# A fused attention and expert kernel: one group of transposes per attention step, ninth key blocks transposed later, separate accumulators for the experts

## The chip, the cores and the metric

The kernel runs on one NeuronCore of a Trainium2 chip. The metric is device time in microseconds of one launch, the median of several runs. TensorE (PE, with its weight loads as PEld), VectorE (DVE), ScalarE (ACT), GpSimd (POOL) and the DMA queue of SyncE (SP) each run their own instruction stream in order and wait for each other by semaphores. Results of TensorE go to PSUM, which has banks of 512 fp32 columns for each of 128 partitions.

## The reference

```python
# attention: q, k, v are [4, 8, 576, 64]
scores = q @ k.T / 8 + bias(log-distance MLP of w1, b1, w2)   # per head
attn = softmax(scores)            # minus row max, over sum + 1e-9
x = (attn @ v) -> [2304, 512]
# 8 experts, every token goes to its argmax expert
h = relu(x[mask] @ w1[e]); y = h @ w2[e]
out[mask] = gate_w * sigmoid(x @ w_output_gate)[e] * y
# gated feed-forward on all tokens
g = x @ w_gate; out = (silu(g) * (x @ w_val)) @ w_out         # d_ff = 1536
```

## The kernel before

The program has four stages, one after the other: the position bias is made and stored to DRAM (to 68 us), attention (68 to 331 us), the experts (331 to 597 us), the feed-forward (597 us to the end). The recording order in the code is the order on each engine; nothing reorders it but TensorE's own pulling ahead of weight loads.

**Attention** runs 16 *units*, a unit being a pair of heads p of a batch b. A unit has five *steps* c = 0 to 4, each for a tile of 128 query rows of both heads; c = 4 has the last 64 rows of both heads in one tile. Keys are 576 = four and a half blocks of 128. Written without head, one step n does this:

- `s_pe` (L242): the scores S of step n, three fp32r products for each half of the keys; for c < 4 two heads in two PSUM tiles of the pool `pS` (tag `S`, two buffers in all), for c = 4 one tile.
- `s_max` (L255, VectorE): scores plus bias from PSUM into the SBUF tile E (tag `ph`, four buffers), with the row minimum of the negated sum; `s_exp` (L260, ScalarE): the exponentials, in place.
- `t_pe` (L279): transposes of E of step n-2 ("old") into the PSUM tile T, two banks, one for each half of the partitions; 64-row transposes in pairs, one pair for each block of 128 columns. `t_ev` (L295): the copy from T into the SBUF tiles `pt`, which the weighted sums read.
- the weighted sums `pv` (L349, from `pv_list`), spread over steps by `PVA` and `PVB`; `bc_recip` (L328) spreads the reciprocal row sums at c = 1 and c = 3; at c = 2 and c = 0 VectorE multiplies (L355).

E has nine blocks of 128 for two heads of 576 columns; the fifth of them (number 4) is the one that holds the end of one head and the beginning of the other, and is written to place 8 of `pt`. Here it is called the ninth block. The order of a step is set by the loop at L860:

```python
            if old:
                t_both(*old, 0)      # first group: blocks 0 to 3, copied by VectorE
            E = ap.tile([128, 2 * S], F32, tag="ph", bufs=4, name="E")
            sc = s_pe(p, b, c)
            if old:
                t_both(*old, 1)      # second group: blocks 5 to 8 and 4, copied by ScalarE
```

Both groups use the same columns of both banks of T, so that the second waits for VectorE's copy of the first and the first of the next step for ScalarE's copy of the second. At c = 4 the ninth block needs a GpSimd copy of 64 columns first (L899).

**The experts** loop over 64 steps: `h_step` (L549) makes hidden values in one bank of T, taken in turn by `t_tile` (L266), ScalarE and VectorE split them into a high and a low part (L558, L559), and `y_step` (L561) multiplies the ones of the step before, 12 matmuls each. On TensorE the order is h(n+1), y(n), h(n+2), y(n+1). In between, as listed per step (`todo`), the weights of the next expert are converted (L517, L519) and the first weights of the feed-forward (L941 to L952). `q_h` (L666) also uses T.

Of the kernel before, what the change touches and what calls it, by code (L numbers as in the profile page):

```python
# [9 lines left out]
F32 = mybir.dt.float32  # L10
F32R = mybir.dt.float32r
# [5 lines left out]
PSUM = bass.MemoryType.PSUM  # L17
# [3 lines left out]
B, H, S, D = 4, 8, 576, 64  # L21
# [87 lines left out]
def body(tc, qt, kt, va, vb, ws, moe_w_gate, moe_w_output_gate, moe_w1, moe_w2, w_gate, w_val, w_out, ctab, cst, cst2, out):  # L109
    nc = tc.nc  # L110
    with ExitStack() as ctx:
        const = ctx.enter_context(tc.tile_pool(name="const", bufs=1))
        dram = ctx.enter_context(tc.tile_pool(name="dram", bufs=1, space=DRAM))
        att = ExitStack()
        pers = ctx.enter_context(tc.tile_pool(name="pers", bufs=1))
        vw = att.enter_context(tc.tile_pool(name="vw", bufs=1))
        ap = att.enter_context(tc.tile_pool(name="att", bufs=1))
        rt = att.enter_context(tc.tile_pool(name="rt", bufs=1))
        pS = att.enter_context(tc.tile_pool(name="pS", bufs=2, space=PSUM))
        pO = att.enter_context(tc.tile_pool(name="pO", bufs=1, space=PSUM))  # L120
# [9 lines left out]
        reps = ap.tile([32, 256], F32, tag="ph", bufs=4, name="reps")  # L130
# [21 lines left out]
        for r in range(4):  # L152
            o = slice(32 * r, 32 * r + 32)
# [86 lines left out]
        pts = {}  # L240
# [22 lines left out]
        tt = pO.tile([128, 2, 512], F32, name="T")  # L263
        turn = [0]

        def t_tile():  # L266
            turn[0] ^= 1
            return tt[:, turn[0] ^ 1]

        def pv_tile(i, name):  # L270
            return pO.tile([128, 512], F32, tag=f"pv{i}", bufs=1, name=name)
# [4 lines left out]
            swap[0] ^= 1  # L276
            return pv_tile(swap[0] ^ 1, name)

        def t_pe(E, c, i):  # L279

            ns = ((0, 1, 2, 3), (5, 6, 7, 8, 4) if c < 4 else (4,))[i]
            for j, n in enumerate(ns):
                for r in range(2):
                    k, o = slice(64 * r, 64 * r + 64), 128 * n + (64 * r if c == 4 and i == 0 else 0)
                    nc.tensor.transpose(tt[:, r, 64 * j:64 * j + 64], E[k, o:o + 128], ident[k, k])  # L287
# [7 lines left out]
        def t_ev(p, b, c, i):  # L295

            pt = pts[p, b][c // 2 if c < 4 else 1]
            if c < 4:
                o, n = 128 * (c % 2), 4 + i
                copy(i, pt[:, 4 * i:4 * i + n, o:o + 128].rearrange("p n (r t) -> p r n t", r=2),  # L300
                     tt[:, :, 0:64 * n].rearrange("p r (n t) -> p r n t", n=n))
            elif i == 0:
                copy(i, pt[:, 0:8, 256:320].rearrange("p (r n) t -> p r n t", r=2), tt[:, :, 0:256].rearrange("p r (n t) -> p r n t", n=4))
            else:
                for r in range(2):
                    k = slice(64 * r, 64 * r + 64)
                    copy(i, pt[k, 8, 256:320], tt[k, r, 0:64])

        def t_both(p, b, c, E, i):
            t_pe(E, c, i)  # L310
            t_ev(p, b, c, i)
# [53 lines left out]
        act = vm[:, 0:1]  # L365
# [140 lines left out]
        def conv_w(raw, f, later=None):  # L506

            a, c = raw
            if f < 4:
                ta = ap.tile([128, 2, 4, 128], F32R, tag="ph", bufs=4, name="w1hl")  # L510
# [299 lines left out]
        def z_mm(cnt):  # L810
            c, k = BLKS[cnt]
            act = ZACT[cnt % len(ZACT)]
            zs = zss.pop(cnt)
            pt = pS.tile([128, 1024], F32, tag="S", name="bps")
            ps = [pt[:, 0:512], pt[:, 512:1024]]
            for gq in range(4):
                nc.tensor.matmul(ps[0][32 * gq:32 * gq + 32, 0:512], w2bd, zs[gq][:, 0:512], start=True, stop=True)
            for gq in range(4):
                nc.tensor.matmul(ps[1][32 * gq:32 * gq + 32, 0:64], w2bd, zs[gq][:, 512:576], start=True, stop=True)
            ob = ap.tile([128, S], F32, tag="ph", bufs=4, name="ob")  # L820
# [38 lines left out]
        sts = {}  # L859
        for n, (ui, c) in enumerate(steps):  # L860
            p, b = units[ui]
            g = 9 * ui + min(2 * c + 1, 8)
            if c == 0:
                if b == 0:
                    xT[p] = pers.tile([128, NTOK], F32, tag=f"xT{p}", name=f"xT{p}")
                    if p + 1 < NP:
                        dmaq += [(9 * ui + BL[i], f) for i, f in enumerate(load_bias(p + 1))]
                if b == 1 and p + 1 < NP:
                    dmaq += [(9 * ui + VL[i], f) for i, f in enumerate(load_v(p + 1, nc.sync))]
                if ui + 2 < len(units):  # L870
                    dmaq += [(9 * ui, f) for f in load_u(*units[ui + 2])]
# [12 lines left out]
            old = prev.pop(0) if len(prev) == 2 else None  # L884
            if old:
                t_both(*old, 0)
            E = ap.tile([128, 2 * S], F32, tag="ph", bufs=4, name="E")
            sc = s_pe(p, b, c)
            if old:
                t_both(*old, 1)  # L890
            fs = pe.pop(n, [])
            for f in fs[0:1]:
                f()
            for hh in range(1 if c == 4 else 2):
                e = E[:, S * hh:S * hh + S]
# [17 lines left out]
            prev.append((p, b, c, E))  # L913
# [390 lines left out]
```

## Time and profile before

| | |
|---|---|
| runs | 1055.15 us median of 3 (1054.14 to 1056.36) |
| profiled execution | 1057.95 us, its span 1056.1 us |
| TensorE busy | 1007.4 us (95%), weight loads 798.8 us (76%) |
| VectorE, ScalarE, GpSimd busy | 574.0 us (54%), 449.8 us (43%), 128.6 us (12%) |
| mean granted clock | 0.987 |

The span runs from the first to the last instruction in the profile. Matmuls overlap in their records, so TensorE's busy share holds time in which it starts nothing; the idle time of the weight loads (PEld), with what ended it, shows these waits better.

### The profile page before, as it was taken

The page shows a single profiled execution, that of the slowest core. Times are in us where ns is not written, and L with a number is a line of the kernel's source. Part 1 is how long each engine was busy: PE and PEld are TensorE (multiplying, and loading weights), DVE is VectorE, ACT ScalarE, POOL GpSimd, SP SyncE. Part 2 cuts the span into 40 slices and gives each one's busy share as a digit, 9 for nine tenths or more (in the row PEclk, how much of TensorE's full clock was granted, in tenths as well). Part 3 has the DMA queues.
Part 4 walks back from the last instruction along what each step waited for, and adds up shares of the span by engine and source line. Part 5 has one row for each costly group of instructions (what it writes and reads, how often), then busy time and mean ns, then how long its engine had stood idle before and what let it go on. Part 6 is the DMA issues. An engine that isn't in the chain of part 4 may idle for free. (4 is left out here: it accounts for less than half of the span.)

```text
span 1056.1 us, 18793 instructions
## 1 busy us (share of the span) xinstructions
PE 1007.4 (95%) x7461; PEld 798.8 (76%) x7461; DVE 574.0 (54%) x1241; ACT 449.8 (43%) x931; POOL 128.6 (12%) x138
## 2 busy tenths in 40 slices
PE   6979999999989999999999899999999999999998
PEld 2346666666657899998988677778888888888897
DVE  8966777677666644444556399962223222322322
ACT  6766777676755433333425355541112111211221
POOL 3662343344220000000000000000000000000000
PEclk9988999999999999999999999999999999999999
DMA  6783233342013042724724555512001000200010
GB/s 190 205 263 118 93 100 98 109 133 93 14 36 116 23 161 102 255 97 129 261 100 146 170 160 179 172 58 70 1 1 52 29 1 1 60 1 0 12 30 20
DMA packets 67755, 101.90 MB, mean 96 GB/s; under 512 B 9136, under 2 KB 37936, under 8 KB 67664
## 3 DMA queue, kind: packets, MB, share of 16 engines
q1 hardware_dynamic: 67504, 100.41, 29.8%
q8 instruction: 59, 0.97, 0.4%
q10 hardware_dynamic: 160, 0.26, 0.1%
q14 instruction: 32, 0.26, 0.1%
HBM read 74.63 MB, written 26.03 MB: 95 GB/s over the span
## 5 line engine op out<-in xcount | busy, mean ns | idle before, releaser
L1199 PE MATMUL v<-x,w 128*128 128x512 f32 (+1 forms) x720 | 161.3, 371 | 3.8 <-DVE w L952 3.8
L1199 PE MATMUL g<-x,w 128*128 128x512 f32 (+1 forms) x720 | 159.9, 371 | 2.3 <-DVE xl L707 2.2
L1199 PEld LDWEIGHTS v<-x,w 128*128 128x128 f32 x720 | 125.3, 189 | 32.0 <-DVE w L952 7.5
L1199 PEld LDWEIGHTS g<-x,w 128*128 128x128 f32 x720 | 127.4, 189 | 27.3 <-ACT x L1154 2.5
L1221 PE MATMUL o<-w,uh 128*128 128x512 f32 x432 | 133.3, 390 | 0.0
L1202 DVE TENSOR_TENSOR t<-g,t 128x512 f32<-128x512 f32 (+1 forms) x60 | 38.2, 636 | 170.1 <-ACT t L1201 170.1
L261 ACT ACTIVATE E<-E,st 128x576 f32<-128x576 f32 x144 | 109.9, 766 | 5.1 <-DVE st L256 4.5
L256 DVE CUSTOM_DVE_ANT_0 E<-S,bias 128x576 f32<-128x576 f32 x128 | 92.0, 755 | 16.2 <-PE S L252 8.0
L1201 ACT ACTIVATE t<-g 128x512 f32<-128x512 f32 (+1 forms) x60 | 33.2, 553 | 153.7 <-PE g L1199 153.7
L349 PE MATMUL pv<-pt,rawv 128*64 128x256 f32 (+1 forms) x640 | 97.6, 425 | 0.0
L1206 ACT ACTIVATE uh<-t 128x512 fp32r<-128x512 f32 (+1 forms) x60 | 35.4, 590 | 145.6 <-DVE t L1203 145.6
L1221 PEld LDWEIGHTS o<-w,uh 128*128 128x128 f32 x432 | 80.3, 188 | 16.1
L287 PEld LDWEIGHTS T<-ident,E 64*128 64x128 f32 x1312 | 55.9, 142 | 46.8 <-ACT pt L291 20.2
L293 DVE COPY pt<-T 128x512 f32<-128x512 f32 x80 | 55.2, 691 | 60.8 <-PE T L287 39.6
L291 ACT ACTIVATE pt<-T 128x640 f32<-128x640 f32 (+1 forms) x96 | 52.2, 543 | 74.9 <-PE T L287 74.7
L1221 PE MATMUL o<-w,ul 128*128 128x512 f32 x216 | 84.0, 389 | 0.0
L287 PE MATMUL T<-ident,E 64*128 64x64 f32 x1312 | 77.1, 238 | 6.6 <-ACT pt L291 1.6
L252 PE MATMUL S<-kh,qz 64*128 64x288 f32 (+1 forms) x576 | 77.3, 322 | 3.7 <-DVE st L256 3.1
L558 ACT ACTIVATE qz<-T 128x288 fp32r<-128x288 f32 x63 | 25.9, 411 | 107.0 <-PE T L556 104.9
L559 DVE SCALAR_TENSOR_TENSOR qz<-T,qz 128x288 fp32r<-128x288 f32 x63 | 28.7, 456 | 72.7 <-ACT qz L558 72.4
L1203 DVE TENSOR_TENSOR t<-v,t 128x512 f32<-128x512 f32 (+1 forms) x60 | 38.3, 638 | 54.4 <-PE v L1199 53.0
L556 PE MATMUL T<-xh,whl 128*128 128x288 f32 x256 | 58.2, 302 | 6.4 <-DVE qz L559 5.1
(245 smaller groups left out, 1655.7 us busy)
## 6 DMA issues: line engine op xcount, KB each, us to landing
raww<-in_moe_w_dram SPq DMA_DIRECT2D x16, 768.0 KB, 6.2
bscr<-ob SPq DMA_DIRECT2D x36, 288.0 KB, 4.0
bias<-bscr SPq DMA_DIRECT2D x16, 576.0 KB, 4.2
rw<-in_w_gate_dram SPq DMA_DIRECT2D x12, 512.0 KB, 3.7
rw<-in_w_val_dram SPq DMA_DIRECT2D x12, 512.0 KB, 3.6
rw<-in_w_out_dram SPq DMA_DIRECT2D x12, 512.0 KB, 3.7
rawq<-in_qt_dram SPq DMA_DIRECT2D x16, 320.0 KB, 3.3
rawk<-in_kt_dram SPq DMA_DIRECT2D x16, 288.0 KB, 3.1
```

Of the source, the lines that this page charges most:

```text
L252: nc.tensor.matmul(t[:, f, 0:288], x[k, a], y[k, o], start=i == 0, stop=i == 2)
L256: nc.vector.tensor_tensor_reduce(out=E.rearrange("p (a b) -> p a b", a=2), in0=ps[:, :, 0:288], in1=bt[p, hh, c].rearrange("p (a b) -> p a ...
L261: nc.scalar.activation(E, E, AF.Exp, bias=st[:, 2 * c + hh:2 * c + hh + 1], scale=-1.0, accum_out=st[:, 10 + 2 * c + hh:11 + 2 * c + hh])
L287: nc.tensor.transpose(tt[:, r, 64 * j:64 * j + 64], E[k, o:o + 128], ident[k, k])
L291: nc.scalar.activation(o, x, AF.Copy)
L293: nc.vector.tensor_copy(o, x)
L349: nc.tensor.matmul(st["ps"][64 * hh:64 * hh + 64, 0:w], vt[p][:, hh, b, c, :], pts[p, b][f][:, c + 4 * hh if c < 4 else 8, :], start=c == ...
L556: nc.tensor.matmul(ps, wa[:, x, k], xs[k][y][:, o], start=k == 0 and i == 0, stop=k == 3 and i == 2)
L1199: nc.tensor.matmul(t, a[:, 128 * k:128 * k + 128], x, start=k == 0 and n == 0, stop=k == 3 and n == 2)
L1202: nc.vector.tensor_tensor(t, ps[0], t, ALU.mult)
L1203: nc.vector.tensor_tensor(t, ps[1], t, ALU.mult)
L1221: nc.tensor.matmul(ops[j][m], u[:, o], w, start=f == 0 and n == 0, stop=f == NF - 1 and n == 2)
```

## The change

Per step the scores now come first, then all transposes of the old step in one group of 16 (c < 4), then the weighted sums. ScalarE's copy of blocks 5 to 8 is recorded right behind the group, VectorE's of blocks 0 to 3 behind `s_max`. The ninth blocks of c = 0 and 1 are transposed in the group of c = 2 (four transposes more) into a second PSUM tile `Tx`, taken from the pool `pS`, since the step at whose place this happens (c = 4) needs only one score tile; those of c = 2 and 3 in the group of c = 4. The GpSimd copy is gone: the ninth block of c = 4 is made by one 64x64 transpose and one 64x64 matmul with the identity. `E` is now allocated behind the transposes, so that four buffers still do; `EB` is 4. Behind attention T is given back and the experts take two separate tiles of one bank each.

```diff
@@ s_pe and transposes of one step
-        def t_pe(E, c, i):
-            ns = ((0, 1, 2, 3), (5, 6, 7, 8, 4) if c < 4 else (4,))[i]
-            for j, n in enumerate(ns):
-                for r in range(2):
...
+        def t_blk(E, t, at, n, shift=0):
+            for r in range(2):
+                k, o = slice(64 * r, 64 * r + 64), 128 * n + shift * r
+                nc.tensor.transpose(t[:, r, at:at + 64], E[k, o:o + 128], ident[k, k])
+
+        def t_pe(c, Es, x):
+            t, E = tb["t"], Es[-1]
+            if c == 2:
+                for i in range(2):
+                    t_blk(Es[i], x, 64 * i, 4)
+            if c < 4:
+                for j, n in enumerate((0, 1, 2, 3, 5, 6, 7, 8)):
+                    t_blk(E, t, 64 * j, n)
+            else:
+                for i in range(2):
+                    t_blk(Es[2 + i], t, 256 + 64 * i, 4)
+                for j in range(4):
+                    t_blk(E, t, 64 * j, j, 64)
+                nc.tensor.transpose(t[0:64, 0, 384:448], E[0:64, 512:576], ident[0:64, 0:64])
+                nc.tensor.matmul(t[64:128, 0, 384:448], E[64:128, 0:64], ident[64:128, 64:128], start=True, stop=True)
...
+                copy(act, pt[c // 2][:, n:n + 4, o:o + 128].rearrange("p n (r t) -> p r n t", r=2),
+                     t[:, :, 64 * n:64 * n + 256].rearrange("p r (n t) -> p r n t", n=4))
+                if c == 2 and not act:
+                    copy(0, pt[0][:, 8].rearrange("p (c r t) -> p r c t", c=2, r=2), x[:, :, 0:128].rearrange("p r (c t) -> p r c t", c=2))
...
         def t_tile():
             turn[0] ^= 1
-            return tt[:, turn[0] ^ 1]
+            if "pool" in tb:
+                return tb["pool"].tile([128, 512], F32, tag="T", bufs=2, name="T")
+            return tb["t"][:, turn[0] ^ 1]
...
-            if old:
-                t_both(*old, 0)
-            E = ap.tile([128, 2 * S], F32, tag="ph", bufs=4, name="E")
             sc = s_pe(p, b, c)
             if old:
-                t_both(*old, 1)
-            fs = pe.pop(n, [])
-            for f in fs[0:1]:
+                x = pS.tile([128, 2, 512], F32, tag="S", name="Tx") if c == 4 else None
+                t_pe(old[3], old[4], x)
+                t_ev(*old[1:4], x, 1)
+            E = ap.tile([128, 2 * S], F32, tag="ph", bufs=EB, name="E")
...
                 s_max(p, hh, c, sc[hh], e, st)
                 s_exp(e, st, hh, c)
-            if c == 4:
-                nc.gpsimd.tensor_copy(E[:, 576:640], E[:, 0:64])
...
+            if old:
+                t_ev(*old[1:4], x, 0)
...
+        pT.close()
+        tb["pool"] = att.enter_context(tc.tile_pool(name="pT2", bufs=1, space=PSUM))
```

On TensorE, at the change from the step c = 4 of one unit to c = 0 of the next, the program before reads so (T transposes, S scores, pv weighted sums, pt the copies; a wait stands behind the first instruction that has it):

```order
L287 MATMUL T<-ident,E 128x64 [waits DVE_49]
L287 MATMUL T<-ident,E 128x64 x9
L349 MATMUL pv<-pt_2882,rawv 64x320 x2
L349 MATMUL pv<-pt_3115,rawv 64x256 [waits Activation_49]
L349 MATMUL pv<-pt_3115,rawv 64x256
L287 MATMUL T<-ident,E 128x64 [waits Activation_49]
L287 MATMUL T<-ident,E 128x64 x7
L252 MATMUL S<-kh,qz_117 128x288 [waits Pool_49]
L252 MATMUL S<-kh,qz_117 128x288 [waits DVE_49]
```

and the changed one so:

```order
L288 MATMUL Tx<-ident,E 128x64 [waits DVE_49]
L288 MATMUL Tx<-ident,E 128x64 x3
L288 MATMUL T<-ident,E 128x64 [waits DVE_49]
L288 MATMUL T<-ident,E 128x64 x15
L364 MATMUL pv<-pt_2892,rawv 64x320 x2
L364 MATMUL pv<-pt_3126,rawv 64x256 [waits Activation_49]
L364 MATMUL pv<-pt_3126,rawv 64x256
L255 MATMUL S<-kh,qz_120 128x288 [waits DVE_49,Pool_49]
L255 MATMUL S<-kh,qz_120 128x288 [waits DVE_49,PE_49]
```

The scores of the next unit stand directly behind the weighted sums, and their second matmul, that of the other head, now waits for VectorE and TensorE, since it takes the buffer that `Tx` had.

On VectorE, the same place (L256 and L259 are `s_max`, L293 and L311 the copies out of T; the second L256 or L259 row is the reading of its minimum), before:

```order
L256 ISA E,st<-S,bias 128x576 [waits PE_49]
L256 ISA st 128x1
L293 COPY pt_2882<-T 128x2x4x64 [waits PE_49,Activation_49]
L256 ISA E,st<-S,biast 128x576 [waits PE_49]
L256 ISA st 128x1
L293 COPY pt_2882<-T 128x2x4x64 [waits PE_49,Activation_49]
```

and changed:

```order
L259 ISA st 128x1
L311 COPY pt_2891<-T 128x2x4x64 [waits Activation_49]
L259 ISA E,st<-S,biast 128x576 [waits PE_49]
L259 ISA st 128x1
L311 COPY pt_2892<-T 128x2x4x64 [waits Activation_49]
L311 COPY pt_2891<-Tx 128x2x2x64
```

VectorE's copy out of T, which stood ahead of `s_max`, stands behind it; it waits for ScalarE alone, so for ScalarE's copy of the same group, which itself waits for the group; and a copy out of `Tx` is new behind it.

On TensorE in the expert stage, the end of an h, the y behind it and the beginning of the next h (L556 and L571 are in `h_step`, L569 and L584 in `y_step`), before:

```order
L556 MATMUL T<-xh,whl 128x288
L569 MATMUL y<-qz_118,w2hl 128x288 [waits Activation_49]
L569 MATMUL y<-qz_118,w2hl 128x288 x11
L556 MATMUL T<-xh,whl 128x288 [waits DVE_49]
L556 MATMUL T<-qz_115,whl 128x288
```

and changed:

```order
L571 MATMUL T<-xh,whl 128x288
L584 MATMUL y<-qz_120,whl 128x288 [waits Activation_49]
L584 MATMUL y<-qz_120,whl 128x288 [waits DVE_49]
L584 MATMUL y<-qz_120,whl 128x288 x10
L571 MATMUL T<-xh,whl 128x288
L571 MATMUL T<-qz_118,whl 128x288
```

The wait for VectorE has moved from the first matmul of h to the second of y.

## Rows read from the trace of the kernel before

**Rows 1.** Window of attention: its us, then busy us (count) of each engine, granted clock, DMA share, GB/s.

```profile
90.00:290.00 200.00, 197.78 (x2374) 133.41 (x2368) 141.86 (x352) 142.46 (x342) 75.34 (x97) 1.00 0.31 94
```

**Rows 2.** Waits of the weight loads, same stretch: total us, times, longest.

```profile
PEld T L287 <- DVE pt L293: 12.0, 52, 0.5
...
PEld T L287 <- POOL rw L323: 4.0, 13, 0.3
```

**Rows 3.** TensorE groups by form, same stretch: busy us, mean ns | idle us before.

```profile
L287 PE MATMUL T<-ident,E 64*128 64x64 f32 x1066 | 60.8, 234 | 2.2 <-DVE pt L293 0.2
```

**Rows 4.** Timeline of one step, c=2, all engines: start, us, engine, line.

```profile
245.88 0.47 PE L287 MATMUL T<-ident,E 64*128 64x64 f32 x8
...
246.16 0.51 PE L252 MATMUL S<-kh,qz 64*128 64x288 f32 x4
...
246.46 0.69 DVE L293 COPY pt<-T 128x512 f32<-128x512 f32 x1 [0.80 <-PE T L287]
...
247.20 0.39 PEld L287 LDWEIGHTS T<-ident,E 64*128 64x128 f32 x10 [0.25 <-DVE pt L293]
247.21 0.52 PE L287 MATMUL T<-ident,E 64*128 64x64 f32 x10
...
247.66 1.30 PE L349 MATMUL pv<-pt,rawv 128*64 128x320 f32 x8
247.77 0.70 ACT L291 ACTIVATE pt<-T 128x640 f32<-128x640 f32 x1 [0.65 <-PE T L287]
```

**Rows 5.** The same timeline: a unit's first row, its step c=4, the next unit's first.

```profile
240.09 0.46 PE L287 MATMUL T<-ident,E 64*128 64x64 f32 x8
...
252.43 0.46 PE L287 MATMUL T<-ident,E 64*128 64x64 f32 x8
...
252.82 0.53 PE L252 MATMUL S<-kh,qz 128*128 128x288 f32 x2
...
253.00 0.69 DVE L293 COPY pt<-T 128x512 f32<-128x512 f32 x1 [1.22 <-ACT E L261]
...
253.80 0.39 PEld L287 LDWEIGHTS T<-ident,E 64*128 64x128 f32 x10 [0.17 <-DVE pt L293]
...
254.25 1.19 PE L349 MATMUL pv<-pt,rawv 128*64 128x320 f32 x8
...
255.38 0.46 PE L287 MATMUL T<-ident,E 64*128 64x64 f32 x8
```

**Rows 6.** ScalarE groups by form, attention (90 to 290 us): busy us, mean ns.

```profile
L291 ACT ACTIVATE pt<-T 128x640 f32<-128x640 f32 x52 | 36.7, 706 | 51.4 <-PE T L287 51.4
...
L337 ACT ACTIVATE rb<-rps 128x256 f32<-128x256 f32 x13 | 5.0, 384 | 0.3
```

**Rows 7.** VectorE groups by form, the same stretch.

```profile
L293 DVE COPY pt<-T 128x512 f32<-128x512 f32 x65 | 44.9, 691 | 49.5 <-PE T L287 33.1 <-ACT E L261 14.9 <-ACT rb L337 1.6
...
L355 DVE TENSOR_TENSOR xT<-pv,rb 128x256 f32<-128x256 f32 x13 | 5.5, 419 | 0.0
```

**Rows 8.** Waits of TensorE, 331 to 600 us: total us, times, longest.

```profile
PE T L556 <- DVE qz L559: 5.1, 4, 2.3
...
PE T L671 <- DVE qs L676: 2.1, 3, 1.0
```

**Rows 9.** Timeline of the expert stage, at its longest waits.

```profile
380.61 0.63 ACT L517 ACTIVATE w2hl<-raww 128x512 fp32r<-128x512 f32 x1 [1.45 <-DMA raww<-in_moe_w_dram]
...
382.39 0.41 PE L556 MATMUL T<-xh,whl 128*128 128x288 f32 x1 [1.30 <-DVE qz L559]
...
437.73 0.40 PE L556 MATMUL T<-xh,whl 128*128 128x288 f32 x1 [1.19 <-DVE qz L559]
...
532.72 0.40 PE L556 MATMUL T<-xh,whl 128*128 128x288 f32 x1 [2.27 <-DVE qz L559]
```

**Rows 10.** Windows at the clock's low stretches, columns as in rows 1.

```profile
312.10:319.00 6.90, 6.70 (x48) 4.41 (x50) 4.07 (x12) 3.84 (x10) 0.00 (x0) 0.51 0.70 216
534.00:537.40 3.40, 3.40 (x17) 3.40 (x16) 1.96 (x4) 0.41 (x1) 0.00 (x0) 0.50 0.85 292
```

More of the change, by code (lines that the diff above doesn't have):

```diff
@@ L35 @@
 LG = (1, 5, 5, 7, 8, 10, 10)
+EB = 4
 N0, PRE, FL, LEAD = 6, 3, 0, 0
@@ L120, in body @@
         pO = att.enter_context(tc.tile_pool(name="pO", bufs=1, space=PSUM))
+        pT = ExitStack()
+        pT1 = pT.enter_context(tc.tile_pool(name="pT1", bufs=1, space=PSUM))
         sched = ExitStack()
@@ L129, in body @@
         w_s = const.tile([32, 10], F32, name="w_s")
-        reps = ap.tile([32, 256], F32, tag="ph", bufs=4, name="reps")
+        reps = ap.tile([32, 256], F32, tag="ph", bufs=EB, name="reps")
         rep_sb, w2rep = reps[:, 0:128], reps[:, 128:256]
@@ L261, in s_exp @@
             nc.scalar.activation(E, E, AF.Exp, bias=st[:, 2 * c + hh:2 * c + hh + 1], scale=-1.0, accum_out=st[:, 10 + 2 * c + hh:11 + 2 * c + hh])
-        tt = pO.tile([128, 2, 512], F32, name="T")
+        tb = {"t": pT1.tile([128, 2, 512], F32, name="T")}
         turn = [0]
@@ L277, in pv_next @@
             return pv_tile(swap[0] ^ 1, name)
-        def t_pe(E, c, i):
-            ns = ((0, 1, 2, 3), (5, 6, 7, 8, 4) if c < 4 else (4,))[i]
-            for j, n in enumerate(ns):
-                for r in range(2):
-                    k, o = slice(64 * r, 64 * r + 64), 128 * n + (64 * r if c == 4 and i == 0 else 0)
-                    nc.tensor.transpose(tt[:, r, 64 * j:64 * j + 64], E[k, o:o + 128], ident[k, k])
+        def t_blk(E, t, at, n, shift=0):
[17 more added lines that the diff above has]
+                nc.tensor.matmul(t[64:128, 0, 384:448], E[64:128, 0:64], ident[64:128, 64:128], start=True, stop=True)
         def copy(act, o, x):
@@ L293, in copy, with t_ev @@
                 nc.vector.tensor_copy(o, x)
-        def t_ev(p, b, c, i):
-            pt = pts[p, b][c // 2 if c < 4 else 1]
+        def t_ev(p, b, c, x, act):
+            t, pt = tb["t"], pts[p, b]
             if c < 4:
[L299 to L303, printed above, removed]
-            else:
[L305 to L311, printed above, removed]
+                o, n = 128 * (c % 2), 4 * act
+                copy(act, pt[c // 2][:, n:n + 4, o:o + 128].rearrange("p n (r t) -> p r n t", r=2),
+                     t[:, :, 64 * n:64 * n + 256].rearrange("p r (n t) -> p r n t", n=4))
+                if c == 2 and not act:
+                    copy(0, pt[0][:, 8].rearrange("p (c r t) -> p r c t", c=2, r=2), x[:, :, 0:128].rearrange("p r (c t) -> p r c t", c=2))
+            elif act:
+                copy(1, pt[1][:, 8, 0:256].rearrange("p (c r t) -> p r c t", c=2, r=2), t[:, :, 256:384].rearrange("p r (c t) -> p r c t", c=2))
+                copy(1, pt[1][:, 8, 256:320], t[:, 0, 384:448])
+            else:
+                copy(0, pt[1][:, 0:8, 256:320].rearrange("p (r n) t -> p r n t", r=2), t[:, :, 0:256].rearrange("p r (n t) -> p r n t", n=4))
         late = []
@@ L509, in conv_w @@
             if f < 4:
-                ta = ap.tile([128, 2, 4, 128], F32R, tag="ph", bufs=4, name="w1hl")
+                ta = ap.tile([128, 2, 4, 128], F32R, tag="ph", bufs=EB, name="w1hl")
                 tb = ap.tile([128, 2, 4, 128], F32R, tag="bias", bufs=4, name="w2hl")
@@ L819, in z_mm @@
                 nc.tensor.matmul(ps[1][32 * gq:32 * gq + 32, 0:64], w2bd, zs[gq][:, 512:576], start=True, stop=True)
-            ob = ap.tile([128, S], F32, tag="ph", bufs=4, name="ob")
+            ob = ap.tile([128, S], F32, tag="ph", bufs=EB, name="ob")
             nc.scalar.activation(ob, pt[:, 0:S], AF.Identity, bias=off8[:, act:act + 1], scale=8.0)
@@ L858, in body @@
         prev = []
-        sts = {}
+        sts, es = {}, {}
         for n, (ui, c) in enumerate(steps):
@@ L884, in body @@
             old = prev.pop(0) if len(prev) == 2 else None
-            if old:
-                t_both(*old, 0)
-            E = ap.tile([128, 2 * S], F32, tag="ph", bufs=4, name="E")
             sc = s_pe(p, b, c)
             if old:
-                t_both(*old, 1)
-            fs = pe.pop(n, [])
-            for f in fs[0:1]:
+                x = pS.tile([128, 2, 512], F32, tag="S", name="Tx") if c == 4 else None
+                t_pe(old[3], old[4], x)
+                t_ev(*old[1:4], x, 1)
+            E = ap.tile([128, 2 * S], F32, tag="ph", bufs=EB, name="E")
+            if c == 0:
+                es[ui] = []
+            es[ui].append(E)
+            for f in pe.pop(n, []):
                 f()
@@ L897, in body @@
                 s_exp(e, st, hh, c)
-            if c == 4:
-                nc.gpsimd.tensor_copy(E[:, 576:640], E[:, 0:64])
-            for f in fs[1:]:
-                f()
+            if old:
+                t_ev(*old[1:4], x, 0)
             if c in (1, 3) and ui:
@@ L912, in body @@
             late.clear()
-            prev.append((p, b, c, E))
+            prev.append((ui, p, b, c, es[ui][0:c + 1]))
             while mq and mq[0][0] <= g:
@@ L1045, in body @@
         a, z = prev
-        t_both(*a, 0)
+        t_pe(a[3], a[4], None)
+        t_ev(*a[1:4], None, 1)
+        t_ev(*a[1:4], None, 0)
         p_recip(sts[15])
@@ L1051, in body @@
         pvs(2)
-        t_both(*a, 1)
         pvs(2)
-        t_both(*z, 0)
+        t_pe(z[3], z[4], None)
+        t_ev(*z[1:4], None, 1)
+        t_ev(*z[1:4], None, 0)
         h_step(mu[0]["ws"], mu[0]["xs"], 0, ps=pS.tile([128, 2, 512], F32, tag="S", name="h0")[:, 0])
-        t_both(*z, 1)
+        pT.close()
+        tb["pool"] = att.enter_context(tc.tile_pool(name="pT2", bufs=1, space=PSUM))
         m_conv(0, 1)
```

## Prediction

> **What bounds the kernel now.** I read the window of attention first, since most of the edits are there [rows 1]: TensorE is busy 197.8 of 200 us, VectorE 141.9 and ScalarE 142.5, and the granted clock is 1.00 (2.4 GHz). So TensorE's stream sets the time, and time is won only where that stream holds a gap. The busy sum hides such gaps, because records of matmuls overlap; the waits of the weight loads show them [rows 2]. In the 13 units of this stretch they wait for VectorE's copy out of T 12.0 us in 52 (four steps a unit), and 4.0 us in 13 at the fifth, c=1, where the row names POOL's `rw`, not the cause by the order of the program, since the transposes there need T's columns too.
>
> A step in detail, c=2 [rows 4]: eight transposes at 245.88, scores at 246.16 (so the group costs the stream 0.28), VectorE's copy 246.46 to 247.15, and only at 247.20 the loads of the second group, after 0.25 idle: the scores are through before the copy is. The sums follow at 247.66, and ScalarE's copy of 640 columns lies beside them, 247.77 to 248.47.
>
> The experts' part of this is the table of TensorE's waits: h waits 5.1 us in 4 for VectorE's split of the h before it, q 2.1 us in 3 for a like split [rows 8].
>
> **The change in attention, per unit.** A unit takes 15.29 us (240.09 to 255.38 [rows 5]).
>
> *Removed: the second group's wait.* Idle of the loads is (12.0 + 4.0) / 13 = 1.23 us a unit. At c=4 it is not this wait: the copy ends at 253.00 + 0.69 = 253.69, before the loads at 253.80 [rows 5], so its 0.17 goes to the change of tile shape and stays; 1.06 are left in four steps. About 0.04 of each is overlapped by the stream's end: gain 0.89. Bounds: 0.7 (if 0.09 of each were overlapped) to 1.06.
>
> *Moved: the transposes' borders.* The number of transposes stays 82 a unit (1066 in 13 units [rows 3]). Eight alone cost 0.28; two more cost 0.52 - 0.47 = 0.05 to 0.06 [rows 4], so 0.03 each, and one group for two saves a border. But the scores now stand behind the weighted sums, whose loads leave them less lead; I count these against each other, ±0.05 a step. At c=4 the border was dearer, 252.43 to 252.82 = 0.39 instead of 0.28 [rows 5]: gain 0.11. Together 1.00.
>
> *Added: a wait at the change of unit.* The scores of the next unit's second head take the buffer of `Tx`, so they wait for VectorE's copy out of it. The chain from the beginning of the group at c=4: 20 transposes, 0.53 + 10 x 0.031 = 0.84; 0.04 to ScalarE (247.73 to 247.77 [rows 4]); its copy of 512 columns, between 0.384 for 256 and 0.706 for 640 [rows 6], 0.60; then, in series because VectorE's copy waits for ScalarE alone, 0.05; 0.69 [rows 7]; the copy of 256 columns out of `Tx`, for which I take the nearest row, a 256-column product of 0.419 [rows 7], 0.42; 0.05 to TensorE. The sum is 2.69, less 0.08, since it is the second matmul that waits: 2.61. TensorE's own work from the same point is 0.77 of transposes (0.45 for ten, 253.80 to 254.25, and ten at 0.031) and 1.13 of sums (254.25 to 255.38 [rows 5]), 1.90. The stall is 0.71. Bounds: 0.28, if ScalarE's copy and VectorE's lay side by side so far that only 0.17 of the first counted, to 1.0, if the `Tx` copy cost as much as the 0.69 of 512 columns. Who is late next: the next `s_max` of head 1, which VectorE has to wait for anyway.
>
> The series has a rule behind it: the Trainium skill, page "PSUM — Partial Sum Buffer", section "PSUM bank collisions raise a hardware error", says that two engines may not touch one bank in the same quarter of the partitions at once, two reads included. It speaks against the change, whose two copies share both banks; by it the 0.60 counts whole. No run here shows an overlap of such copies.
>
> *Added: the odd pair at c=1.* One transpose becomes a 64x64 matmul with another tile shape. No row shows it; its price lies between two more transposes (0.06) and the dearest border seen, 0.39; the nearest is the extra of a group's border, 0.28 - 8 x 0.031 = 0.03, or the 0.17 idle at a change of tile shape [rows 5]. I take 0.06 + 0.17 = 0.23, both kinds of price together.
>
> *At nothing.* GpSimd's copy and its reader go; GpSimd is 75.3 of 200 us busy [rows 1]. ScalarE copies 512 columns for 640, off the path. VectorE's main copy moves behind `s_max`: the weighted sums that need it are a step away, and the next group waits for it only if it ends later than 3 us after the group before; by the chain (0.84 + 0.04 + 0.60 + 0.05 + 0.69 = 2.2) it does not. If that cover went, each 0.1 would cost 0.5 a unit. `s_max` at c=4 and c=1 now waits for the first pair of transposes, for its E buffer, some 0.1 late beside slack on VectorE. No DMA moves.
>
> Sum a unit: -1.00 + 0.71 + 0.23 = -0.06; for 16 units -1.0, which I round to -0.8. Ends: about ±0.3 a unit, ±4.8 us.
>
> Behind attention, the router works with T too; its groups lose a wait or two and gain serial copies: 0, ±1. The stretch at half clock there (0.51 from 312.1 to 319.0 [rows 10]) I leave as it is.
>
> **The change in the experts.** With one tile of two banks, the first matmul of h waits for the split of the h before it, though it writes the other bank; this shows in the order as the wait of the first matmul. With two tiles that wait stands at the second matmul of y, which needs that split itself, 12 matmuls x 0.13 = 1.57 us later. So a wait up to 1.57 goes whole: 1.30 at 382.39 and 1.19 at 437.73 go, of the 2.27 at 532.72 1.57 go [rows 9], and the fourth of the 5.1 is what remains, 0.3: 4.4 together. Behind the 2.27 the granted clock is 0.50 from 534.0 to 537.4 [rows 10], and behind 1.30 and 1.19 it is not: I expect that the low stretch goes with the long wait, 3.4 x 0.5 = 1.7. Of q's 2.1 I take two thirds, 1.4, since these have no y of full length behind them. Sum 7.5. Ends: 4.4 - 1.6 = 2.8 if the waits come again in y, and 8.2 with all of q's. Nothing hides behind h in exchange: the matmul that then waits first is y's, and behind it the next h, as now.
>
> Total: -0.8 - 7.5 = -8.3. The profiled execution took 1057.95 (its span 1056.1 and 1.85 around it, which the change does not touch), so the sum gives 1049.65; that execution is 0.27% above the median of 1055.15, and put on the median it is 1046.9 us, a ratio of 0.992.
>
> **The rivals.**
>
> *A, attention wins as well.* If ScalarE's copy and VectorE's overlap, or the stall is else near its lower bound of 0.28, a unit wins 0.43 more: 16 x 0.43 = 7, so 1040. For: nothing in VectorE's 142 of 200 us forbids an earlier copy. Against: the wait for ScalarE alone, in the order.
>
> *B, the experts' waits only move.* The split of h is late because ScalarE is: its conversion of weights at 380.61 waited 1.45 us for a DMA [rows 9]. If the weights set the pace, a shorter wait in h becomes a wait for the weights, and the gain is 2.8: 1055.15 - 0.8 - 2.8 = 1051.5. Against: in a wait of 1.3 the split itself is what ends last, and after it TensorE has all its weights.
>
> *C, slower: the clock falls at the change of unit.* 20 transposes, then a gap of 0.7 us, stand there sixteen times; if the granted clock went to 0.5 behind each for a stretch like the one at 534.0, 3.4 us, each would cost 1.7, sixteen 27 less the 8.3: 1074. It decides for slower from 7 falls on (7 x 1.7 - 8.3 = +3.6). For: that stretch followed a gap of 2.27. Against: gaps of 1.30 and 1.19 had no fall behind them, and 82 transposes in each 15.29 us leave the clock at 1.00 [rows 1]. The Trainium skill, page "TensorE: Matmul & The Clock Gate", section "Part 4: PE-mode transpose", says that full clock does not engage for transposes, which do not count as busy in the same way; by that rule 20 of them in a row would bring the fall nearer. The trace of before does not show it in groups of 8 and 10.
>
> *D, no change to speak of.* If the stall and the odd pair are dearer by 0.4 to 0.5 a unit (a `Tx` copy near 0.7, the odd pair at its 0.39, and borders that cost 0.05 a step), attention loses 6 to 7 and takes the experts' gain: 1053 to 1056.
>
> **How the numbers follow.** Forecast 0.62, A 0.12, B 0.10, D 0.10, C 0.06. A measurement of this kernel can tell about 0.2%, 2.1 us. Faster by more than that (under 1053.0) are the forecast, A and, B being at 1051.5, nearly all of B: 0.83, the rest of B's chance going to no change: 0.11 with D. Slower: 0.06. The range: low end 1041 (attention's 4.8 and 1 of the router), high end 1053 (attention's other end, 4, and experts of 5.4); it leaves out C, D and most of A, some 2 in 10.
>
> **What the profile after would show.** Right: in 90 to 290 no idle of the loads behind the scores; one row of some 16 transposes a step; at each change of unit the second score matmul waits about 0.7 for VectorE's copy out of `Tx`, with ScalarE's copy, VectorE's and that one in series ahead of it; a unit of 15.2 to 15.3 us; no waits of h for its split and at most 0.7 of y's; clock at 1.00 to 290 and no low stretch after 530. Wrong: a group of T that waits for VectorE at other steps; the granted clock under 1.00 in attention; waits for weights that fill the experts' gain.

## The result, and the profile after

The changed kernel takes 1041.72 us (median; 1041.17 to 1042.37) against 1055.12 of the kernel before: ratio 0.987, 95% interval 0.9855 to 0.989, 13.4 us faster. Its profiled span is 1040.5 for 1056.1, 15.6 less; that is 2.2 more than between the medians, since the profiled execution of the kernel before took 1057.95, 2.8 above its median. The forecast was 1046.9 within 1041 to 1053: the direction held, the range held by 0.7 us, and the gain is 1.6 times the one forecast.

Laying the two traces against each other at the same matmuls says where it went. At the first y the changed kernel is 7.9 us ahead, at the first matmul of the feed-forward 15.75, at the end 15.6. So attention and router gave 7.9 (forecast 0.8), the experts 7.9 (forecast 7.5), the feed-forward nothing.

Windows of the changed kernel, columns as in [rows 1]: attention, the stretch where before ran at half clock [rows 10], and a new low stretch in the experts.

```profile
90.00:290.00 200.00, 193.71 (x2424) 138.83 (x2422) 142.90 (x370) 135.48 (x345) 75.83 (x88) 1.00 0.30 94
312.00:319.00 7.00, 6.70 (x90) 4.76 (x90) 5.62 (x14) 6.12 (x17) 0.00 (x0) 1.00 0.95 284
474.04:477.45 3.41, 3.11 (x16) 3.05 (x15) 0.68 (x5) 0.00 (x0) 0.13 (x1) 0.50 0.29 27
```

Attention's clock is at 1.00 as before; its TensorE busy time is lower (193.7 for 197.8 [rows 1]) though more matmuls start in it (2424 for 2374). The low stretch at 312 is not there, nor the one at 534; one at 474 is. Over the whole traces before has 27.3 us at half clock, the changed kernel 20.5, so 6.8 x 0.5 = 3.4 of the 15.6 us are clock and 12.2 are work. Without it attention and router gave 4.5, since the 3.4 of the stretch at 312 lies in them.

TensorE's waits, whole run (total, times, longest):

```profile
PE S L255 <- DVE pt L311: 6.4, 15, 0.9
...
PE y L584 <- DVE qz L574: 0.9, 2, 0.5
...
PE y L584 <- ACT qz L573: 0.4, 1, 0.4
```

The rows of y answer to [rows 8]: 5.1 us of h and 2.1 of q are gone, 1.3 of y stand there. The row of the scores is new: 15 times they wait for VectorE's copy at the change of unit.

Timeline of the step c=2, to lay beside [rows 4]:

```profile
243.06 0.53 PE L255 MATMUL S<-kh,qz 64*128 64x288 f32 x4
...
243.96 0.65 PE L288 MATMUL T<-ident,E 64*128 64x64 f32 x16
...
244.54 1.30 PE L364 MATMUL pv<-pt,rawv 128*64 128x320 f32 x8
...
244.65 0.60 ACT L309 ACTIVATE pt<-T 128x512 f32<-128x512 f32 x1 [0.59 <-PE T L288]
...
245.51 0.69 DVE L311 COPY pt<-T 128x512 f32<-128x512 f32 x1
...
245.77 0.53 PE L255 MATMUL S<-kh,qz 64*128 64x288 f32 x4
```

Scores from 243.06 to 243.96 take 0.90, where before took 1.05 from its first score to the second group (246.16 to 247.21); 16 transposes take 0.58 (243.96 to 244.54), where 18 took 0.28 + 0.45 = 0.73; the sums 1.23, as before. The step is 2.71 for 3.01.

Timeline of a unit's c=4 and the beginning of the next one:

```profile
233.87 0.51 PE L255 MATMUL S<-kh,qz 128*128 128x288 f32 x2
...
234.83 0.34 PE L288 MATMUL Tx<-ident,E 64*128 64x64 f32 x4
...
235.01 0.67 PE L288 MATMUL T<-ident,E 64*128 64x64 f32 x16
235.15 0.76 DVE L259 CUSTOM_DVE_ANT_0 E<-S,biast 128x576 f32<-128x576 f32 x1 [1.27 <-PE Tx L288]
...
235.60 1.19 PE L364 MATMUL pv<-pt,rawv 128*64 128x320 f32 x8
235.71 0.60 ACT L309 ACTIVATE pt<-T 128x512 f32<-128x512 f32 x1 [0.94 <-PE T L288]
...
236.34 0.69 DVE L311 COPY pt<-T 128x512 f32<-128x512 f32 x1 [0.42 <-ACT pt L309]
...
236.72 0.40 PE L255 MATMUL S<-kh,qz 64*128 64x288 f32 x1
...
236.95 0.41 DVE L311 COPY pt<-Tx 128x256 f32<-128x256 f32 x1
...
237.51 0.49 PE L255 MATMUL S<-kh,qz 64*128 64x288 f32 x3 [0.39 <-DVE pt L311]
...
240.87 0.56 PE L288 MATMUL T<-ident,E 64*128 64x64 f32 x11
...
241.68 1.08 PE L364 MATMUL pv<-pt,rawv 128*64 128x256 f32 x8
...
248.90 0.51 PE L255 MATMUL S<-kh,qz 128*128 128x288 f32 x2
```

A unit is 15.03 (233.87 to 248.90), in the median of the steady units 15.04 for 15.29. The forecast's chain is here link by link: ScalarE's copy 235.71 to 236.31, VectorE's at 236.34, the one out of `Tx` at 236.95, and the second score matmul at 237.51, 2.68 after the group's first transpose (forecast 2.61). The first one stands at 236.72, so the sums were through then.

### The profile page after: what moved, and what is told of

It is laid out like the page before. It is cut to its first block, busy times and chain, and to the rows that moved or that the text cites. A ratio compares the mean times of both kernels' runs of the same rounds, so it can differ in the third digit from the quotient of the medians.

```text
span 1040.5 us, 18771 instructions
## 1 busy us (share of the span) xinstructions
PE 995.6 (96%) x7477; PEld 802.3 (77%) x7477; DVE 574.5 (55%) x1257; ACT 439.7 (42%) x931; POOL 123.9 (12%) x122
## 5 line engine op out<-in xcount | busy, mean ns | idle before, releaser
L259 DVE CUSTOM_DVE_ANT_0 E<-S,bias 128x576 f32<-128x576 f32 x128 | 91.9, 755 | 47.4 <-PE S L255 24.3
L364 PE MATMUL pv<-pt,rawv 128*64 128x256 f32 (+1 forms) x640 | 95.5, 419 | 0.0
L255 PE MATMUL S<-kh,qz 64*128 64x288 f32 (+1 forms) x576 | 85.3, 328 | 10.5 <-DVE pt L311 6.4
L255 PEld LDWEIGHTS S<-kh,qz 64*128 64x128 f32 (+1 forms) x576 | 58.7, 191 | 36.5 <-issue 22.7
L309 ACT ACTIVATE pt<-T 128x512 f32<-128x512 f32 (+1 forms) x96 | 46.2, 499 | 76.4 <-PE T L288 64.5
L311 DVE COPY pt<-T 128x512 f32<-128x512 f32 x80 | 54.9, 687 | 7.7 <-ACT pt L309 7.7
L571 PE MATMUL T<-xh,whl 128*128 128x288 f32 x256 | 57.5, 300 | 1.4 <-ACT whl L532 0.7
L584 PE MATMUL y<-qz,whl 128*128 128x288 f32 x384 | 56.8, 296 | 1.3 <-DVE qz L574 0.9
```

The costliest lines, as they stand in the source:

```text
L255: nc.tensor.matmul(t[:, f, 0:288], x[k, a], y[k, o], start=i == 0, stop=i == 2)
L259: nc.vector.tensor_tensor_reduce(out=E.rearrange("p (a b) -> p a b", a=2), in0=ps[:, :, 0:288], in1=bt[p, hh, c].rearrange("p (a b) -> p a ...
L364: nc.tensor.matmul(st["ps"][64 * hh:64 * hh + 64, 0:w], vt[p][:, hh, b, c, :], pts[p, b][f][:, c + 4 * hh if c < 4 else 8, :], start=c == ...
L571: nc.tensor.matmul(ps, wa[:, x, k], xs[k][y][:, o], start=k == 0 and i == 0, stop=k == 3 and i == 2)
L584: nc.tensor.matmul(hbuf["y"][d // 2][:, d % 2, 0:288], wb[:, x, d], t[:, y:y + 288], start=f == 0 and i == 0, stop=(one or f == 7) and i == 2)
```

## The experiments

All ratios are to the kernel before, run beside on the same chip. *Unit* is the median distance from c=4 to c=4, read as above.

**The experts alone.** The kernel before with the separate tiles:

```diff
-        tt = pO.tile([128, 2, 512], F32, name="T")
+        tt = pT1.tile([128, 2, 512], F32, name="T")
...
+            if "pool" in tb:
+                return tb["pool"].tile([128, 512], F32, tag="T", bufs=2, name="T")
             return tt[:, turn[0] ^ 1]
...
         t_both(*z, 1)
+        pT.close()
+        tb["pool"] = att.enter_context(tc.tile_pool(name="pT2", bufs=1, space=PSUM))
```

> The kernel before, with nothing but the two separate tiles of one bank each in the expert stage; attention as before. Theory (the wait of h for the split of the h before it goes, and q's with it): the prediction's terms, 4.4 + 1.7 + 1.4 = 7.5 us, so about 1047.6; the aligned traces of before and after say 7.9 between the first y and the first g. Rival (the conversion of weights sets the pace, so the waits only move to y): 2.8 us, about 1052.3. In the profile: no wait of a first h matmul for a split, waits of y for its split under 0.8.

Measured: 1045.11 us, 0.9896 (0.9881 to 0.9911), 11 us faster, unit 15.29. Its trace has 17.1 us at half clock for 27.3, worth 5.1; the span is 13.5 shorter, so the edit is worth 8.4. The only wait of its y (total, times, longest):

```profile
PE y L574 <- DVE qz L564: 0.5, 1, 0.5
```

So 2.27 became 0.5, by the 1.57 and a little more, and 1.30, 1.19 and 0.3 went whole. The theory stands; in this kernel the rival doesn't.

**Attention alone.** The changed kernel with one tile for the experts:

```diff
-            if "pool" in tb:
-                return tb["pool"].tile([128, 512], F32, tag="T", bufs=2, name="T")
...
-        pT.close()
-        tb["pool"] = att.enter_context(tc.tile_pool(name="pT2", bufs=1, space=PSUM))
```

> The changed kernel with one tile of two banks in the experts as before, so only attention's part of the change is left. The prediction's terms for attention give -0.8 us, 1054.3. The units of the two traces, 15.04 for 15.29 us, give 16 x 0.245 = 3.9 and about 0.9 more at the first units: 4.8, 1050.3. If attention and experts add up, this and the kernel with the experts alone make 13.4 us together. In the profile: units of 15.04, and the waits of h for its split back, about 5 us.

Measured: 1051.25 us, 0.9959 (0.9943 to 0.9976), 4.3 faster, unit 15.04. The span is 7.7 shorter, of which 3.4 are clock (20.5 us low for 27.3), so 4.3 are work. The two halves nearly add up: 8.4 and 4.3 alone make 12.7, and together they give 12.2. Its waits of h and q:

```profile
PE T L568 <- DVE qz L571: 6.1, 3, 2.6
PE T L683 <- DVE qs L688: 2.1, 3, 1.0
```

Q's 2.1 are those of [rows 8]; h's are 6.1 for 5.1, though nothing in the experts differs: the 1.19 of 437.73 is now 2.6, and the fourth wait, of 0.31, is gone. The first is the rival "waits only move" at one place: TensorE arrives there 8.4 us earlier, and ScalarE's conversion of the weights only 7.0 (426.88 for 433.91), which is the 1.4 more of wait.

**The copy out of Tx first.**

```diff
             if c < 4:
                 o, n = 128 * (c % 2), 4 * act
+                if c == 2 and not act:
+                    copy(0, pt[0][:, 8].rearrange("p (c r t) -> p r c t", c=2, r=2), x[:, :, 0:128].rearrange("p r (c t) -> p r c t", c=2))
                 copy(act, pt[c // 2][:, n:n + 4, o:o + 128].rearrange("p n (r t) -> p r n t", r=2),
                      t[:, :, 64 * n:64 * n + 256].rearrange("p r (n t) -> p r n t", n=4))
-                if c == 2 and not act:
-                    copy(0, pt[0][:, 8].rearrange("p (c r t) -> p r c t", c=2, r=2), x[:, :, 0:128].rearrange("p r (c t) -> p r c t", c=2))
```

> The changed kernel with VectorE's two copies at c=4 in the other order: out of Tx first, then the main copy. Theory (the next unit's second score matmul waits for Tx's copy because it stands behind the main copy, which waits for ScalarE): the copy out of Tx lies in VectorE's idle time before ScalarE's copy ends, the stall of 0.66 to 0.76 goes at 15 changes of unit: 10 to 11.4 us, 1030 to 1032. Rival (the scores are held by something else there, or the main copy, 0.1 later, holds the next group instead): 1037 to 1042. In the profile: no wait of the scores for VectorE's copy, units of about 14.3.

Measured: 1029.34 us, 0.9746 (0.9731 to 0.9762), unit 14.37. Timeline at the same place:

```profile
254.81 0.34 PE L288 MATMUL Tx<-ident,E 64*128 64x64 f32 x4
...
255.12 0.76 DVE L259 CUSTOM_DVE_ANT_0 E<-S,biast 128x576 f32<-128x576 f32 x1 [1.27 <-PE Tx L288]
...
255.57 1.19 PE L364 MATMUL pv<-pt,rawv 128*64 128x320 f32 x8
255.68 0.60 ACT L309 ACTIVATE pt<-T 128x512 f32<-128x512 f32 x1 [0.94 <-PE T L288]
...
255.80 0.42 DVE L311 COPY pt<-Tx 128x256 f32<-128x256 f32 x1
...
256.31 0.69 DVE L311 COPY pt<-T 128x512 f32<-128x512 f32 x1
```

The copy out of `Tx` fits between `s_max` and ScalarE's end, and the main copy starts where it did, 0.03 behind ScalarE's. The unit is 0.67 shorter: that is the stall. At 15 changes it makes 10 of the 12.4 us between the medians; the profiled executions, 14.5 us apart, differ by 5.1 us of clock as well (10.2 us at half clock for 20.5).

**The copy out of Tx twice.** Its line stands twice:

```diff
                 if c == 2 and not act:
                     copy(0, pt[0][:, 8].rearrange("p (c r t) -> p r c t", c=2, r=2), x[:, :, 0:128].rearrange("p r (c t) -> p r c t", c=2))
+                    copy(0, pt[0][:, 8].rearrange("p (c r t) -> p r c t", c=2, r=2), x[:, :, 0:128].rearrange("p r (c t) -> p r c t", c=2))
```

> The changed kernel with VectorE's copy out of Tx made twice, one behind the other. Theory (this copy is the last link of the chain that holds the next unit): each change of unit is longer by one copy, 0.41 us, 15 x 0.41 = 6.2 us, 1047.9. Rival (it is hidden beside TensorE's sums): 1041.7, no change. In the profile: the wait of the scores for VectorE's copy longer by 0.4, 1.1 us.

Measured: 1049.46 us, 0.9934 (0.9919 to 0.9949), 0.6% slower than the change, unit 15.51, 0.47 more for a copy of 0.41. The last link of the chain is on the path with its whole length.

**No 64x64 pair.**

```diff
-                nc.tensor.transpose(t[0:64, 0, 384:448], E[0:64, 512:576], ident[0:64, 0:64])
-                nc.tensor.matmul(t[64:128, 0, 384:448], E[64:128, 0:64], ident[64:128, 64:128], start=True, stop=True)
+                t_blk(E, t, 384, 4)
...
+            if c == 4:
+                nc.gpsimd.tensor_copy(E[:, 576:640], E[:, 0:64])
```

with ScalarE's last copy in two halves, as it was.

> The changed kernel with GpSimd's copy of 64 columns back, so that the ninth block of c=4 is an ordinary pair of transposes; no 64x64 pair. Theory (the odd pair costs its change of tile shape, 0.23 a unit): 16 x 0.23 = 3.7 us less than the change, 1038.0; the group at c=1 then takes about 0.58 as at c=2, not 0.81. Rival (the group's length at c=1 comes from elsewhere, or GpSimd's copy is late and the group waits for it): 1041.7 or more.

Measured: 1035.54 us, 0.9811 (0.9792 to 0.9831), unit 14.83: 0.21 less, as costed. 14 units make 3; where the other 3 of the 6 us lie is not shown. The profiled executions are 3.5 us apart, 1.7 of them clock (17.1 us at half clock for 20.5).

**Both.**

> Both at once: the copy out of Tx first, and no 64x64 pair. If the two add up: 1029.3 - 3.7 = 1025.6, units of about 14.14. Rival (without the stall GpSimd, which then has less time between steps, or VectorE holds a group): 1029 or more. A candidate for the best version.

Measured: 1026.71 us, 0.9729 (0.9709 to 0.9749), unit 14.16, 0.88 less than the change: 0.67 and 0.21 add up. It is the fastest kernel here, 29 us below the one before.

**The group cut in two.** On the kernel with the copy out of `Tx` first, half of the transposes, half of the sums, and again:

```diff
-                t_pe(old[3], old[4], x)
+                fs = pe.pop(n, [])
+                t_pe(old[3], old[4], x, (0,))
+                for f in fs[0:1]:
+                    f()
+                t_pe(old[3], old[4], x, (1,))
                 t_ev(*old[1:4], x, 1)
+                pe[n] = fs[1:]
```

> The kernel with the copy out of Tx first (1029.3), and each group of transposes cut in two halves around half of the weighted sums; same transposes, same copies behind the whole group, no wait added for a copy. It prices a border between transposes and other matmuls by itself. Theory (attention gained more than forecast because one group has fewer borders than two, 0.08 a step at c=2): a border pair costs 0.05 to 0.10, 80 steps, 4 to 8 us, 1033 to 1037. Rival (the borders cost nothing, as the forecast counted them against each other, and the gain was a larger wait): 1029. If ScalarE's copy, now 0.65 later, holds the next group: over 1045.

Measured: 1057.22 us, 1.0007 (0.9995 to 1.0019): all of the gain gone. A step, c=0:

```profile
231.92 0.46 PE L288 MATMUL T<-ident,E 64*128 64x64 f32 x8
...
232.31 0.65 PE L369 MATMUL pv<-pt,rawv 128*64 128x256 f32 x4
...
232.89 0.33 PEld L288 LDWEIGHTS T<-ident,E 64*128 64x128 f32 x8 [0.39 <-issue]
232.90 0.46 PE L288 MATMUL T<-ident,E 64*128 64x64 f32 x8
...
233.29 0.65 PE L369 MATMUL pv<-pt,rawv 128*64 128x256 f32 x4
...
233.87 0.54 PE L255 MATMUL S<-kh,qz 64*128 64x288 f32 x4
```

No group of transposes waits for a copy, so the third case is not it. One wait is new, though: at c=2 the first sums wait for ScalarE's copy `rb` out of the PSUM tile that they take, 2.2 us in 12 from 92 to 285 us.

```profile
238.18 0.40 PE L288 MATMUL T<-ident,E 64*128 64x64 f32 x8
...
238.77 0.76 PE L369 MATMUL pv<-pt,rawv 128*64 128x320 f32 x4 [0.19 <-ACT rb L357]
```

From the group to the sums it is 0.59 here, and 0.34 at c=3 (241.44 to 241.78). So 0.25 of the 1.73 a unit (16.10 for 14.37) is this wait, and about 1.48 are left for the cut, 0.30 a step, three times the upper end of what I expected. At c=0, above, eight transposes take 0.39 before sums follow, not 0.28, and the halves of the sums 0.58 or 0.59, where the whole took 1.01. The loads of the second half stand idle 0.39 until the sums in front are through.

**Three blocks first.** The kernel before, with VectorE's copy shorter:

```diff
-            ns = ((0, 1, 2, 3), (5, 6, 7, 8, 4) if c < 4 else (4,))[i]
+            ns = (((0, 1, 2), (3, 5, 6, 7, 8, 4)) if c < 4 else ((0, 1, 2, 3), (4,)))[i]
...
-                o, n = 128 * (c % 2), 4 + i
+                o, n = 128 * (c % 2), 3 + 3 * i
```

with the place in `pt` to match.

> The kernel before with one edit: the first group has the blocks 0 to 2 and the second 3, 5 to 8 and 4, so that VectorE copies 384 columns, not 512, and ScalarE 768, not 640; the order and the number of transposes stay. It prices the wait of the second group for VectorE's copy by itself. VectorE's copy takes 0.691 for 512 and 0.414 for 256, so 0.55 for 384. Theory (the wait is on the path one for one at c=0, 2 and 3, not at c=4): 0.14 x 3 = 0.42 a unit, 16 units, 6.7 us less than before, about 1049.4. Rival (most of that idle time is a border between tile shapes, and the wait only coincides): under 2 us less. If ScalarE's longer copy holds the next group: no gain or a loss.

Measured: 1049.56 us, 0.9941 (0.9922 to 0.996), unit 14.90, 0.39 less. The step c=2:

```profile
246.23 0.40 PE L287 MATMUL T<-ident,E 64*128 64x64 f32 x6
...
246.44 0.52 PE L252 MATMUL S<-kh,qz 64*128 64x288 f32 x4
...
246.74 0.56 DVE L293 COPY pt<-T 128x384 f32<-128x384 f32 x1 [0.31 <-ACT E L261]
...
247.35 0.45 PEld L287 LDWEIGHTS T<-ident,E 64*128 64x128 f32 x12
...
247.87 1.30 PE L349 MATMUL pv<-pt,rawv 128*64 128x320 f32 x8
```

VectorE's copy takes 0.56, and from the first score to the second group it is 0.91 for 1.05: 0.14, one for one. But no idle is left in front of these loads and 0.91 is the 0.90 of the changed kernel: the wait was worth 0.14 to 0.15 a step, not the 0.21 I had read out of 0.25 idle.

**The gap made longer.** The copy out of `Tx` four times, and in a second kernel three times:

```diff
                 if c == 2 and not act:
-                    copy(0, pt[0][:, 8].rearrange("p (c r t) -> p r c t", c=2, r=2), x[:, :, 0:128].rearrange("p r (c t) -> p r c t", c=2))
+                    for _ in range(4):
+                        copy(0, pt[0][:, 8].rearrange("p (c r t) -> p r c t", c=2, r=2), x[:, :, 0:128].rearrange("p r (c t) -> p r c t", c=2))
```

> The changed kernel with VectorE's copy out of Tx made four times, so that TensorE stands still for about 1.9 us at each change of unit, behind the 20 transposes. Theory (a gap of this size there leaves the granted clock at 1.00): 3 x 0.41 x 15 = 18.5 us, 1060. Rival C of the prediction, moved up (the clock falls behind such gaps, 1.7 us for each stretch): up to 15 x 1.7 = 26 more, 1068 to 1086, with low stretches in the window of attention.

> The changed kernel with the copy out of Tx made three times: TensorE stands still for about 1.5 us at each change of unit. It lies between the kernel with two copies (1.1 us, no low stretch from 90 to 290 us) and that with four (1.9 us, five low stretches there). Without falls of the clock: 1041.7 + 2 x 0.41 x 15 = 1054.0, and the granted clock 1.00 from 90 to 290; if the clock falls as with four copies, about 8 more, 1062.

Measured: four times 1070.63 us, 1.015 (1.0125 to 1.0175); three times 1055.83, 0.9996 (0.9984 to 1.0008). The window 90 to 290 us of the kernel with two copies:

```profile
90.00:290.00 200.00, 189.68 (x2352) 135.74 (x2350) 145.27 (x373) 133.50 (x338) 72.32 (x82) 1.00 0.31 94
```

and its scores' waits, 90 to 285 us:

```profile
PE S L255 <- DVE pt L311: 10.2, 12, 0.9
```

The window of the kernel with three copies:

```profile
90.00:290.00 200.00, 184.28 (x2273) 132.30 (x2272) 145.22 (x373) 127.75 (x324) 69.75 (x80) 0.98 0.31 94
```

and its waits, 90 to 290 us:

```profile
PE S L255 <- DVE pt L311: 15.7, 12, 1.3
```

The windows of the kernel with four, one of its low stretches first:

```profile
122.70:126.10 3.40, 3.26 (x31) 2.99 (x33) 1.44 (x4) 0.60 (x2) 0.00 (x0) 0.51 0.02 5
90.00:290.00 200.00, 180.55 (x2158) 130.34 (x2155) 143.24 (x364) 121.84 (x309) 66.12 (x75) 0.95 0.30 94
```

and its waits, 90 to 290 us:

```profile
PE S L255 <- DVE pt L311: 19.4, 11, 1.8
```

The granted clock there is 1.00, 0.98 and 0.95. All three have a low stretch around the window's beginning (from 88 to 90 us on); behind it none follows at 0.85 of idle a change (10.2 / 12), one at 1.3, five at 1.8. With four copies 37.5 us in all are at half clock for the change's 20.5, 8.5 us of the 29. So rival C does happen here, with longer gaps; with the change's own, 6.4 us in 15 or 0.43 each, no low stretch stands from 90 to 290 us.

## Why the prediction was right, and where its sizes were off

**The wait removed** was there and went, but it was mis-sized: -0.89 forecast, -0.69 measured. The stretch from the first score to the next group went from 1.05 to 0.90 at c=0, 2 and 3, and from 1.14 to 0.90 at c=1. The step that failed is "about 0.04 of each is overlapped": idle of the weight loads runs while the last scores still stream, and the shorter copy shows that 0.10 to 0.11 of the 0.25 was no loss, not 0.04.

**The borders** are the term that made the difference: -0.11 forecast, about -0.44 measured (what the unit's -0.25 leaves beside -0.69, 0.67 and 0.21; rows show some of it, at the two places named next, and the rest is a remainder). "I count these against each other, ±0.05 a step" failed: two groups became one, at c=2 that gave 0.15 (0.73 to 0.58), of which 0.06 are two transposes moved to another step; where the reciprocal sums stand ahead (c=3), 128-row scores behind them came 0.41 after, 64-row transposes 0.54, 0.13 more. The group cut in two shows that a border of transposes is anything but free, though its 0.30 is for a place between sums, not for the one removed.

**The stall** was forecast 0.71, and is 0.67 by the copy's other order; the series of copies is in the timeline. **The odd pair** was forecast 0.23, and is 0.21: the group at c=1 took 0.81 with it (240.87 to 241.68), that at c=2 0.58. Rival A, the overlap of the two copies, did not come: attention won more for another reason. The rule that the forecast cites from the Trainium skill (page "PSUM — Partial Sum Buffer", section "PSUM bank collisions raise a hardware error") fits the row, VectorE's copy 0.03 behind ScalarE's end. The row doesn't test it, since the program's own semaphore makes that wait, and what an overlap would do no run here shows.

**The experts.** The h waits gave about 4.2 in the changed kernel (forecast 4.4), by another way than forecast. Where one went whole it gave more than its length: between the aligned traces 1.57 for 1.30, 0.57 for 0.31, and with the experts alone 1.45 for 1.19. Whether the 0.31 went by the separate tiles is not shown, since it went with attention alone too. And where the weights were late it gave nearly nothing, 0.14 for the 1.19, in the timeline of y (idle and releaser at the end):

```profile
429.06 0.40 PE L584 MATMUL y<-qz,whl 128*128 128x288 f32 x1 [0.38 <-ACT qz L573]
429.86 0.93 PE L584 MATMUL y<-qz,whl 128*128 128x288 f32 x5 [0.40 <-DVE qz L574]
...
523.69 1.59 PE L584 MATMUL y<-qz,whl 128*128 128x288 f32 x10 [0.54 <-DVE qz L574]
```

The wait of 1.19 has become 0.38 for ScalarE's part and 0.40 for VectorE's, so rival B holds at one of four places. Both parts of the split stand behind ScalarE's conversion of the next weights, which waits for a DMA, before and after:

```profile
433.91 0.63 ACT L517 ACTIVATE w1hl<-raww 128x512 fp32r<-128x512 f32 x1 [1.70 <-DMA raww<-in_moe_w_dram]
```

```profile
426.04 0.63 ACT L532 ACTIVATE w1hl<-raww 128x512 fp32r<-128x512 f32 x1 [3.28 <-DMA raww<-in_moe_w_dram]
```

TensorE is 9.4 us ahead there, the conversion 7.9. How far ahead TensorE is doesn't decide it: the kernel with two copies, 0.8 us ahead, has the same waits (0.30 and 0.40, the conversion at 434.64 behind 3.21 of waiting), and the fastest one, 24.0 ahead, has none there (409.99, behind 1.81). It is whether these weights keep up. The last row is what is left of the 2.27: 0.54, where 2.27 less 1.57 would leave 0.70. **Q** was mis-sized: 1.4 forecast, 3.5 measured between the traces; all three waits went, not two thirds. That the sum for the experts came out (7.5 for 7.9) is luck in part: the 1.7 of clock in it didn't come, and q gave 2.1 more. In attention the two misses, 0.20 less from the wait and 0.33 more from the borders, are of opposite sign too.

**The clock** I had left as it was at 312 and expected to be whole behind 534. Both low stretches went, one at 474 came, 3.4 us in sum; one at the beginning of the feed-forward (598.9 before, 583.3 after) stayed, against "no low stretch after 530". Which ones come I can't say from these runs: the kernel with the experts alone has none in the experts, attention alone one at 477, behind the same waits, and the 17 runs of the kernel before beside the last two experiments have mean granted clocks of 0.986 to 0.991, by themselves some 5 us apart. So it stays open, and it is not shown that the change brought these 3.4 us. On transposes, the trace doesn't bear out that they bring a fall nearer, as the forecast took from the Trainium skill (page "TensorE: Matmul & The Clock Gate", section "Part 4: PE-mode transpose"): 20 in a row left the granted clock at 1.00 from 90 to 290 us, and stretches at half clock came only as the idle time behind them grew to 1.3 and 1.8.

Open too is what makes the expert's weights late: their DMA was issued at 429.29 before and at 419.84 after, earlier by the lead, and the conversion began 4.6 us behind that before and 6.2 after.

## What to carry to other kernels

When work of one kind stands in two groups in a step, price the borders from rows as well as the wait between them; here they were worth about 0.44 of 1.13 a unit, and cutting a group cost 0.30 a step where the wait had cost 0.15. A copy that frees a buffer which the next matmul takes goes ahead of a copy that waits for another engine: that one exchange was worth 0.67 a unit, where all edits of attention together had brought 0.25. Two buffers in one tile are one buffer to whatever waits by tiles.

## What the runs showed of the hardware that was not expected

- A wait that goes gives its idle time and 0.26 to 0.27 more (1.30 to 1.57, 1.19 to 1.45, 0.31 to 0.57): the idle is counted from the end of the last record, while a following matmul starts 0.13 behind the start of one that lasts 0.30, which hides 0.17, and the one after the first behind a wait starts 0.23 behind it (437.73 to 437.96), 0.10 more than 0.13.
- Cutting a group of 16 transposes by four sums costs about 0.30 a step beside the one wait that it brings.
- A gap of 0.85 us at each change of unit left the clock at 1.00 from 92 to 290 us, one of 1.8 us brought five stretches of 3.4 us at half clock.
